# Later loads of elements 1 to 3 held behind the first weight matrix, element 1's keys on GpSimd's queue, and a new order for every engine

## The chip, the cores and the metric

The kernel runs on one core of one Trainium2 chip. The metric is the device time of one execution in microseconds (us); the time of the kernel before is the median of three executions, 109.86 us (109.25 to 112.44). One execution was also recorded by the hardware profiler; the times inside a run are counted from the start of its span.

The core has TensorE (PE, matrix products; PEld is its loading of weights), VectorE (DVE), ScalarE (ACT), GpSimd (POOL) and SyncE (SP, which here only issues transfers). Each engine takes its own instructions strictly in their written order. Transfers are issued from SP, ACT and POOL and are carried by the same 16 DMA engines.

## What is computed

Four batch elements, four heads, 1088 positions, head size 32. Polynomial attention without a softmax, then a two-layer network on the 4352 resulting rows:

```python
def phi(x):                                   # 32 -> 64 features
    a = np.einsum('rd,bhsd->bhsr', S1, x)     # r = 8
    b = np.einsum('rd,bhsd->bhsr', S2, x)
    return np.einsum('bhsi,bhsj->bhsij', a, b).reshape(*x.shape[:-1], r * r)
kv  = np.einsum('bhsf,bhsd->bhfd', phi(k), v)
z   = np.sum(phi(k), axis=2)
num = np.einsum('bhsf,bhfd->bhsd', phi(q), kv)
den = np.einsum('bhsf,bhf->bhs', phi(q), z)[..., None] + 1e-06
x   = (num / den) as rows [4352, 128]         # heads side by side
out = np.maximum(x @ w_in, 0.0) ** 2 @ w_out  # 128 -> 2048 -> 128
```

## The kernel before, in words

**The work and its names.** Every piece of work is an `op` of a small planner in the kernel file (class `Plan`), with a name, an engine (or two that could do it), a modelled duration and what it reads and writes. For the four elements b = 0 to 3:

- `ld kin_x.b`, `ld qin_x.b`, `ld vin_x.j` load keys, queries and values. Each of the three has two buffers, so element 2 reuses element 0's. Element 0 comes in pieces (`ld k0.0`, `ld k0.1`, `ld k0.r`, `ld q0.0` to `.2`, `ld vin_0.0` to `.3`, `.r0`, `.r1`); elements 1 to 3 have one transfer of 544 KB for the keys, one for the queries, and four for the values. In this text k1, q1 and v1.0 to v1.3 are those of element 1, and so on.
- `kT`, `K1`, `kab`, `kp`: keys transposed (DVE), multiplied with S1 and S2 (PE), turned back (DVE), and the 64 products per position formed in five pieces `kpb.0` to `.8` (POOL or DVE). `z`, `zs`, `Wc_ps`, `Wc` make the denominator's weights, `kvb.0` to `.8` the sum over positions, `kvs`, `KVT`, `KV4T`, `KV` bring it into shape.
- `qT`, `qpr`, `qpc`, `qa`, `qc`, `ac`, `den`, `rec`, `a'`, `qo`, `qd` do the same for the queries, scaled by one over the denominator; `x...` (PE) multiplies them with the sum and `xT...` copies the result, in bf16, to where the network reads it.
- The network runs over ten chunks of rows: `0a` and `0b` of 256 rows, `1` to `7` of 512, `8` of 256 (the two last positions of every group). A chunk is 8 groups of `F1 n.g` (x @ w_in, PE), `relu n.g` (ACT, a few on DVE), 4 of `sq n.g2` (square, DVE, a few on ACT) and 4 of `F2 n.g2` (@ w_out, PE); the 256-row chunks have half as many, each as large. `osb` copies the result out of PSUM and `st o...` stores it. Chunks 0a, 0b and 1 need element 0, chunks 2 and 3 element 1, 4 and 5 element 2, 6 and 7 element 3.

**What sets the order.** `ORDER` is a list of the numbers of all ops, written out by hand (found by a search), and `ALT` names the ops that run on their second engine. `Plan.run` walks the list with its modelled durations only to give out the PSUM buffers (two of two banks, `h`; four of one bank, `t`); each engine then executes its ops in the order of the list, and waits on the chip are set by the data. A real extra wait comes only where `behind` is set: the transfer is then not issued before the named one has landed (line 971). A load's `reads=["gate"]` orders it in the planner alone.

**The places that the change touches.** `load_whole` (line 288) loads the keys and queries of elements 1 to 3, all from SP, with no `behind`. `load_v` (line 294) loads the values; those of element 1 come from POOL, those of 2 and 3 from SP (`loads`, line 930). w_in and w_out (line 364 and the next) are loaded on POOL, after the copy `gate` (line 363), which waits for `ld q0.0`. They are read as f32 (1 MB each) and land as bf16 (512 KB). Line 109 and those around it model a transfer's landing, lines 891 to 903 store chunks 0a and 0b, 0a in four transfers (`HALVES`).

**The order around the start**, decoded from the list, up to the first network chunks:

```
SP    ld k0.0 | k0.1 | k0.r | q0.0 | v0.0 | v0.1 | v0.2 | q0.1 | q0.2 | k1 | k2 | q1 | v2.1 | k3 | q2 | ...
POOL  ... S2r | v0.r0 | v0.r1 | gate | ld w_in | kp0.2 | S2b | kp0.4 | ld v1.0 | kp0.8 | ld v1.3 | ld w_out |
      ld v1.2 | ld v1.1 | a'1 | qo1.0 | qo1.1 | kp1.2 | kp1.6 | kp1.4 | kp1.8 | kp2.2 | kp1.0 | ...
DVE   m4 | kT0.0 | m2 | Wab | W4 | kT0.1 | kab0.0 | kT0.r | kab0.1 | E1 | kab0.r | qT0.0 | mh | kp0.0 | kp0.6 | zs0 |
      qo0.0 | qT0.1 | qT0.2 | ac0.0 | den0.0 | qTr0 | rec0.0 | kvs0 | kT1 | ac1 | den1 | rec1 | xT0.0 | kab1 | kT2 |
      zs1 | qd1.0 | Wc1 | qd1.1 | qT1 | kab2 | xT1.A | ...
PE    S12T | K1 0.0 | K1 0.1 | K1 0.r | z0 | qpr0.0 | kv0.0 | kv0.2 | Wc_ps0 | kv0.4 | c0.0 | kv0.6 | qpr1.0 | kv0.8 |
      qpr1.2 | qoT0.0 | qpr1.4 | KVT0 | R0.0 | x0.0 | K1 1 | KV4T0 | F1 0a.2 | F1 0a.0 | z1 | F1 0a.1 | Wc_ps1 |
      F1 0a.3 | K1 2 | x1 | qpce1 | qpre1 | F1 0b.1 | F2 0a.0 | F1 0b.0 | F2 0a.1 | ... | xe1 | F1 1.6 | F2 1.0 |
      F1 1.7 | F1 1.4 | kv2.0 | ...
ACT   ... | qa0.0 | Wc0 | kvs40 | qp0.0 | qab1 | KV0 | Rs0.0 | KV40 | relu 0a.2 | relu 0a.0 | relu 0a.1 | relu 0a.3 |
      sq 0a.0 | sq 0a.1 | relu 0b.1 | relu 0b.0 | osb0a | relu 0b.3 | relu 0b.2 | sq 0b.1 | ...
```

Ahead of the first `F1` the PE also runs filler products (line 962), put in where the planner sees idle time.

Of the kernel before, what the change touches and what calls it, by code (L numbers as in the profile page):

```python
# [23 lines left out]


HOP, FIX, TAIL, SWITCH = 0.06, 1.4, 0.6, 0.1
RATE = 235.0
OVER = {"PE": 0.15, "DVE": 0.08, "ACT": 0.1, "POOL": 0.03}


class Plan:
# [35 lines left out]
    def run(self, slots, t0=0.7):  # L67
        free = {e: t0 for e in ("PE", "ACT", "DVE", "POOL", "SP")}
        held = {"DVE": [], "POOL": []}
        dmat = {}  # L70
        lane = {"HW": [], "SW": []}
        pool = {kind: [(0.0, (kind, i)) for i in range(n)] for kind, n in slots.items()}
        users, last, was = {}, {}, False
        for o in self.ops:
            for t in o.uses:
                users[t] = users.get(t, 0) + 1
        assert sorted(ORDER) == list(range(len(self.ops)))
        self.order = [self.ops[i] for i in ORDER]
        for o in self.order:
            e, d = o.eng[ALT.get(o.n, 0)]  # L80
            full = o.name[0] == "F"
            s = free[e] + (SWITCH if e == "PE" and full != was else 0.0)
            was = full if e == "PE" else was
            for p in o.preds:
                s = max(s, p.end + (HOP if p.eng[0][0] != e or p.dma is not None else 0.03))
            for t in o.allocs:
                x = min(pool["h"] + pool["t"] if t.kind == "r" else pool[t.kind])
                t.kind, t.i = x[1]
                pool[t.kind].remove(x)
                s = max(s, x[0] + HOP if x[0] else 0.0)  # L90
            if e in o.port:
                other = held["DVE" if e == "POOL" else "POOL"][-14:]
                if e == "POOL" and held["DVE"]:
                    s = max(s, held["DVE"][-1][1] + HOP)
                near = 0.06 if e == "DVE" else 0.0
                while any(a <= s + near and s < b - 1e-9 for a, b in other):
                    s = next(b for a, b in other if a <= s + near and s < b - 1e-9)
                held[e].append((s, s + d))
            if o.dma is not None:
                l = lane["SW" if e == "POOL" else "HW"]  # L100
                s = max(s, l[-8] if len(l) > 7 else 0.0)
                if e == "POOL":
                    held[e].append((s, s + 0.75 * d))
            o.eng, o.start, o.end = [(e, d)], s, s + d
            free[e] = s + d - (OVER.get(e, 0.0) if o.dma is None else 0.0)
            if o.dma is not None:
                q_, x_ = ("SW", "HW") if e == "POOL" else ("HW", "SW")
                begin = max(dmat.get(q_, 0.0), o.end + (FIX if o.pri is None else 1.0 if e != "POOL" else 2.2))
                shared = min(max(dmat.get(x_, 0.0) - begin, 0.0), 2 * o.dma) / 2
                dmat[q_] = begin + o.dma + shared  # L110
                dmat[x_] = dmat.get(x_, 0.0) + shared
                o.end = dmat[q_] + TAIL
                lane[q_].append(o.end)
            for t in o.uses:
                users[t] -= 1
                last[t] = max(last.get(t, 0.0), s + d)
                if users[t] == 0:
                    pool[t.kind].append((last[t], (t.kind, t.i)))
        return self.order
# [8 lines left out]
HOOK = {"1": ("0a", 3), "e1": ("1", 4), "e2": ("3", 4), "e3": ("5", 4), "8": ("6", 4)}  # L128
FINE = ("8",)
FILL = 0.12  # L130
HALVES = ("0a",)
ORDER = [
# [21 lines left out]
]  # L154
ALT = {
# [3 lines left out]
}  # L159


# [1 line left out]
def kernel(  # L163
# [33 lines left out]
    S2r = T("S2r", [128, D])  # L197
# [10 lines left out]
    w_in = T("w_in", [128, d_ff], BF16)  # L208
# [36 lines left out]
    P = Plan()  # L245
# [33 lines left out]
    def rows(x, b):  # L279
        return x[b].rearrange("h (t j) d -> (h t) j d", j=NJ)  # L280
# [4 lines left out]
    def keys3(rg, b):  # L285
        return [f"{rg(b)[1]}.{x}" for x in ("0", "1", "2" if rg is qin else "r")]

    def load_whole(x, b, rg):
        t, key = rg(b)
        load("SP", f"ld {key}.{b}", t, rows(x, b), 557, keys3(rg, b), ["gate"])  # L290

    JK = [0, 9, 18, 26]

    def load_v(b, eng):
        t, key = vin(b)
        vr = v[b].rearrange("h (t j) d -> t h j d", j=NJ)
        for j4 in range(4):
            j0, n = (8 * j4, 8) if b == 0 else (JK[j4], 9 if j4 < 2 else 8)
            l = load(eng if isinstance(eng, str) else eng[j4], f"ld {key}.{j4}", t[32 * j4 : 32 * j4 + 32, :, :n, :].rearrange("p h m d -> p h (m d)"),
                 vr[:, :, j0 : j0 + n, :].rearrange("t h m d -> t h (m d)"), 16.4 * n,  # L300
                 [f"{key}.{j4}"] + ([f"{key}.r{j4}"] if n == 9 else []), ["gate"] if b else [f"{K0k}.0"] if j4 == 3 else [], first=b == 0)
            if b == 0 and j4 == 3:
                l.behind = P.w[f"{K0k}.0"]
        if b == 0:
            for g in range(2):
                load("POOL", f"ld {key}.r{g}", t[32 * g : 32 * g + 32, :, 8, :], vr[:, :, 32 + g, :], 16, [f"{key}.r{g}"], first=True)
# [623 lines left out]
    def loads(b):  # L930
        if b < B:
            load_whole(k, b, kin)
            load_whole(q, b, qin)
            load_v(b, "POOL" if b == 1 else "SP")

    first_part(x0, "x0.0")
    token_major("1")
# [64 lines left out]
```

## Time and profile before

| | |
|---|---|
| Median of three executions | 109.86 us (109.25 to 112.44) |
| The profiled execution, its own time | 110.45 us |
| its span, from first to last instruction | 107.9 us |
| granted TensorE clock, mean | 0.99 |
| busy: PE / DVE / ACT / POOL | 97.8 / 89.4 / 80.0 / 29.9 us |
| DMA: moved in all | 10.22 MB, mean 95 GB/s |
| first F1 product | at 17.50 us |
| last F2 product ends | at about 102.1 us |

How to read it: the view by groups has, for each line of the kernel and shape, the busy time, the mean of one, and the idle time ahead of it with what ended it. The timeline gives start and duration in time order; a row with several instructions gives the time from the first one's start to the last one's end. The chain of waits follows the work that ended last back through what released each step. In the view of the DMA queues, the hardware queue q1 is SP's, q10 is ACT's, and the software queue q0 is POOL's. A matmul's duration is that of one pipelined product, so the time of a group on PE is read from its neighbours' starts.

### The profile page before, as it was taken

How to read it: one execution, taken by the hardware profiler on the slowest of the kernel's cores; microseconds unless marked ns; L12 is line 12 of the kernel's file. 1: busy time of each engine (PE TensorE's matmuls, PEld its weight loads, DVE VectorE, ACT ScalarE, POOL GpSimd, SP SyncE). 2: the span in 40 equal slices, each digit the busy share in tenths (PEclk: the TensorE clock that was granted, in tenths of full speed). 3: DMA queues.
4: the chain of work that ended last, by engine and by line, in shares of the span. 5: the costliest groups of instructions: out<-in, count | busy, mean ns of one | idle time of the engine just before them, and what ended most of it. 6: DMA issues, size and time to landing. Idle time of an engine off the chain costs nothing.

```text
span 107.9 us, 3883 instructions
## 1 busy us (share of the span) xinstructions
PE 97.8 (91%) x1676; PEld 71.9 (67%) x1676; DVE 89.4 (83%) x137; ACT 80.0 (74%) x99; POOL 29.9 (28%) x44
## 2 busy tenths in 40 slices
PE   7886999799999998999999999999999999999800
PEld 5545776549777575666886786788568688889600
DVE  1588479899999799979998998998889999979600
ACT  3230063999999988979999699999887799678600
POOL 7339906999189562000003000000000000000000
PEclk9999999999999999999999999999999999999996
DMA  1999999991029921000000122000032001200242
GB/s 37 255 211 337 308 304 233 301 282 61 6 74 223 260 70 51 0 6 3 0 0 6 55 79 67 0 6 0 7 87 82 0 0 51 76 0 11 80 110 52
DMA packets 9360, 10.22 MB, mean 95 GB/s; under 512 B 848, under 2 KB 8064, under 8 KB 9344
## 3 DMA queue, kind: packets, MB, share of 16 engines
q1 hardware_dynamic: 8448, 8.13, 26.8%
q0 software_dynamic: 576, 1.66, 6.9%
q10 hardware_dynamic: 320, 0.20, 1.0%
q8 instruction: 13, 0.21, 0.8%
q14 instruction: 3, 0.02, 0.1%
HBM read 8.80 MB, written 2.23 MB: 102 GB/s over the span
## 4 chain that ended last, share of the span: by engine, by line
PE 63%; ACT 14%; DMA 8%; DVE 5%; issue 3%; ACTq 0%
PE h L801 22%; PE t L837 21%; ACT r L813 10%; PE t L448 6%; DMA vin<-in_v_dram 5%; DMA kin<-in_k_dram 3%; PE h L652 2%; DVE g L826 2%; ACT osb L268 2%; ACT g L826 2%; PE h L553 2%; PE h L486 1%; PE h L680 1%; PE t L684 1%; ACT r L807 1%
## 5 line engine op out<-in xcount | busy, mean ns | idle before, releaser
L813 ACT ACTIVATE r<-h 128x1024 bf16<-128x1024 f32 x63 | 61.3, 1024 | 6.8 <-PE h L801 6.4
L837 PEld LDWEIGHTS <-g 128*128 128x128 bf16 x544 | 33.1, 98 | 5.5 <-DVE g L809 0.3
L837 PE MATMUL t<-w_out,g 128*128 128x128 bf16 x544 | 36.0, 219 | 0.1
L826 DVE TENSOR_TENSOR g<-r 128x2048 bf16<-128x2048 bf16 x29 | 34.5, 1206 | 0.8 <-ACT r L813 0.5
L801 PE MATMUL h<-xT,w_in 128*128 128x512 bf16 (+1 forms) x112 | 29.8, 370 | 0.6 <-ACT r L813 0.4
L801 PEld LDWEIGHTS <-w_in 128*128 128x128 bf16 x160 | 18.7, 148 | 7.8 <-issue 4.2
L499 POOL TENSOR_TENSOR kp<-kab 128x512 f32<-128x512 f32 x12 | 12.6, 1073 | 17.0 <-DVE g L826 17.0
L633 DVE STREAM_TRANSPOSE qd<-qo 128x1024 f32<-128x1024 f32 (+1 forms) x7 | 7.9, 1144 | 0.0
L448 PE MATMUL t<-kp,vin 128*32 128x64 f32 (+1 forms) x288 | 6.9, 223 | 1.1 <-DMA vin<-in_v_dram 0.9
L826 ACT ACTIVATE g<-r 128x2048 bf16<-128x2048 bf16 x4 | 7.6, 1922 | 0.1
L448 PEld LDWEIGHTS t<-kp,vin 128*32 128x32 f32 (+1 forms) x288 | 4.8, 109 | 4.2 <-issue 2.0
L962 PE MATMUL t<-const-bfloat16-1.0 128*128 128x256 bf16 x35 | 6.7, 326 | 0.8 <-PEq L986 0.8
L801 PE MATMUL h<-x0r,w_in 128*128 128x256 bf16 (+1 forms) x32 | 6.7, 333 | 0.0
L652 PE MATMUL h<-qd,KV 32*32 32x256 f32 (+2 forms) x160 | 6.3, 342 | 0.2 <-ACT r L813 0.2
L652 PE MATMUL t<-qd,KV 32*32 32x256 f32 (+2 forms) x160 | 6.5, 343 | 0.0
L814 DVE TENSOR_SCALAR r<-h 128x1024 bf16<-128x1024 f32 x4 | 4.9, 1224 | 1.1 <-PE h L801 0.7
L962 PEld LDWEIGHTS <-const-bfloat16-1.0 128*128 128x128 bf16 x35 | 3.7, 118 | 2.4 <-issue 1.3
L652 PEld LDWEIGHTS h<-qd,KV 32*32 32x32 f32 x160 | 3.4, 103 | 2.2 <-ACT r L813 0.7
L718 DVE TENSOR_TENSOR qo<-qaq,qaf 128x1024 f32<-128x1024 f32 x4 | 4.7, 1218 | 0.0
L479 DVE STREAM_TRANSPOSE kT<-kin 128x1088 f32<-128x1088 f32 x3 | 3.9, 1287 | 0.0
L526 DVE STREAM_TRANSPOSE qT<-qin 128x1024 f32<-128x1024 f32 x3 | 3.6, 1204 | 0.0
L268 ACT COPY osb<-t 128x512 f32<-128x512 f32 (+2 forms) x6 | 2.7, 466 | 0.9 <-PE t L837 0.9
(125 smaller groups left out, 99.8 us busy)
## 6 DMA issues: line engine op xcount, KB each, us to landing
out_dram<-osb SPq DMA_DIRECT2D x29, 64.0 KB
kin<-in_k_dram SPq DMA_DIRECT2D x3, 544.0 KB
qin<-in_q_dram SPq DMA_DIRECT2D x3, 544.0 KB
vin<-in_v_dram SPq DMA_DIRECT2D x7, 128.0 KB
vin<-in_v_dram SPq DMA_DIRECT2D x4, 144.0 KB
kin<-in_k_dram SPq DMA_DIRECT2D x2, 256.0 KB
w_in<-in_moe_w_in_dram POOLq DMA_DIRECT2D x1, 512.0 KB, 10.2
w_out<-in_moe_w_out_dram POOLq DMA_DIRECT2D x1, 512.0 KB, 10.2
```

Source lines behind the costliest of these rows:

```text
L268: op(e, 0, lambda en: act.copy(o(), i()) if en == "ACT" else dve.tensor_copy(o(), i()), reads, writes, name)
L448: pe.matmul(pb(tv)[32 * h : 32 * h + 32, :64], V[:Pn, h, m, :], kp_[:Pn, m, h].rearrange("p i j -> p (i j)"), start=(m == 0), stop=(m == 8 ...
L499: return (pool if e == "POOL" else dve).tensor_tensor(out=kp_[:, 2 * u : 2 * u + 2].rearrange("p m h i j -> p (m h) i j"), in0=x, in1=y, o ...
L633: op("DVE", DVT(256 * G), lambda e: dve.transpose(qd_[:, g0 : g0 + G].rearrange("p g f t -> p (g f t)"), qo_[:, :G].rearrange("p g h x y - ...
L652: pe.matmul(bank[32 * h : 32 * h + 32, :n], KV4[rg if b is None else b][rows, y, 32 * h : 32 * h + 32], qd_[rows, :G, 2 * h + y, :], start ...
L718: return (pool if e == "POOL" else dve).tensor_tensor(out=qo_.rearrange("p g h i j -> p (g h) i j"), in0=x_, in1=y_, op=ALU.mult)
L801: pe.matmul(hv()[:, x], w_inv[:, ct], X, start=True, stop=True)
L813: lambda e, hv=hv, Rv=Rv, own=own: act.activation(Rv[:, own], hv(), ACTF.Relu) if e == "ACT"
L814: else dve.tensor_scalar_max(Rv[:, own], hv(), 0.0),
L826: lambda e, R=R, G=G: dve.tensor_mul(G, R, R) if e == "DVE" else act.activation(G, R, ACTF.Square),
L837: pe.matmul(tb[o.i][:, x : x + 128], Gv[:, y, tt * 128 : tt * 128 + 128], w_out[:, ct], start=(ct == 0 and x == 0), stop=(ct == CT - 1), s ...
L962: pe.matmul(pb(fill)[:, :256], one.to_broadcast([128, 128]), one.to_broadcast([128, 256]), start=True, stop=True)
```

## The change

Four things change. (1) Element 1's keys go from SP's queue to POOL's, in the list between `gate` and `ld w_in`. (2) Every other later load of keys, queries and values (q1, v1, and all of elements 2 and 3) gets `behind = w_in`: the queue that issues it stands until w_in has landed. v1.0 to v1.2 go from POOL's queue to SP's; v1.3 stays on POOL's. (3) The planner adds a measured lateness to the first loads' modelled landings, and chunk 0a's store goes out in two transfers in place of four. (4) `ORDER` and `ALT` are new.

```diff
+LATE = (("ld k0.r", 1.0), ("ld S2r", 1.0), ("ld q0.0", 0.6), ("ld vin_0.", 0.6), ("ld q0.1", 0.3))
...
-                o.end = dmat[q_] + TAIL
+                o.end = dmat[q_] + TAIL + next((x for a, x in LATE if o.name.startswith(a)), 0.0)
...
-HALVES = ("0a",)
+HALVES = ()
 ORDER = [
...
     def load_whole(x, b, rg):
         t, key = rg(b)
-        load("SP", f"ld {key}.{b}", t, rows(x, b), 557, keys3(rg, b), ["gate"])
+        l = load("POOL" if x is k and b == 1 else "SP", f"ld {key}.{b}", t, rows(x, b), 557, keys3(rg, b), ["gate"] if x is k and b == 1 else ["w_in"])
+        if x is not k or b > 1:
+            l.behind = P.w["w_in"]
...
-                 [f"{key}.{j4}"] + ([f"{key}.r{j4}"] if n == 9 else []), ["gate"] if b else [f"{K0k}.0"] if j4 == 3 else [], first=b == 0)
+                 [f"{key}.{j4}"] + ([f"{key}.r{j4}"] if n == 9 else []), ["w_in"] if b else [f"{K0k}.0"] if j4 == 3 else [], first=b == 0)
             if b == 0 and j4 == 3:
                 l.behind = P.w[f"{K0k}.0"]
+            elif b:
+                l.behind = P.w["w_in"]
...
-            load_v(b, "POOL" if b == 1 else "SP")
+            load_v(b, ("SP", "SP", "SP", "POOL") if b == 1 else "SP")
```

The new list, decoded in the same way:

```
SP    ld k0.0 | k0.1 | k0.r | q0.0 | v0.0 | v0.1 | v0.2 | q0.1 | q0.2 | (w_in landed) k2 | q1 | k3 | v1.0 | v1.1 | q2 |
      v2.3 | v1.2 | v2.0 | v2.2 | v3.0 | st o0a.0 | ...
POOL  ... S2r | v0.r0 | v0.r1 | gate | ld k1 | ld w_in | S2b | kp0.6 | ld w_out | kp0.8 | qo1.1 | qo1.0 | kp1.2 | kp1.4 |
      kp1.6 | kp1.0 | (w_in landed) ld v1.3 | kp2.6 | kp1.8 | kp2.4 | ...
DVE   m4 | m2 | kT0.0 | W4 | E1 | Wab | kT0.1 | mh | kab0.0 | kT0.r | kab0.1 | kab0.r | qT0.0 | kp0.0 | kp0.2 | zs0 | kp0.4 |
      qo0.0 | qT0.1 | qT0.2 | ac0.0 | den0.0 | rec0.0 | kT1 | ac1 | den1 | rec1 | a'1 | xT0.0 | qTr0 | kab1 | qd1.1 | qd1.0 |
      kT2 | zs1 | xT1.A | kab2 | qT1 | sq 0a.1 | zs2 | kT3 | ...
PE    S12T | K1 0.0 | K1 0.1 | K1 0.r | z0 | qpr0.0 | kv0.0 | Wc_ps0 | kv0.2 | kv0.4 | c0.0 | qpr1.0 | kv0.6 | qpr1.2 | kv0.8 |
      qpr1.4 | KVT0 | qoT0.0 | KV4T0 | R0.0 | x0.0 | K1 1 | F1 0a.1 | F1 0a.3 | z1 | F1 0a.0 | F1 0a.2 | x1 | K1 2 | F1 0b.2 |
      Wc_ps1 | z2 | F1 0b.0 | F2 0a.0 | ... | xe1 | F1 1.6 | F2 1.0 | F1 1.7 | F1 2.1 | F2 1.1 | F1 2.0 | kv2.0 | ...
ACT   ... | qa0.0 | Wc0 | kvs0 | kvs40 | qab1 | KV0 | qp0.0 | Rs0.0 | KV40 | relu 0a.1 | relu 0a.3 | relu 0a.0 | relu 0a.2 |
      sq 0a.0 | xT1.B1 | relu 0b.2 | xT1.B0 | Wc1 | relu 0b.0 | relu 0b.3 | sq 0b.1 | ...
```

Ops that change their engine. From ACT to DVE: sq 0a.1, sq 1.1, relu 5.4, 6.1 and 7.2, osb3, osb4, and seven smaller copies. From DVE to ACT: sq 1.0, relu 5.7, 6.3, 6.6 and 7.7, osb1, and eleven smaller copies (among them both `xT1.B`, Wc1, Wc2, kvs41, xTe1.A). From POOL to DVE: kp0.2, kp0.4, a'1, a'e2. From DVE to POOL: kp0.6, a'e1.1, qoe2.0, qoe3.0. PE's work is the same, in another order.

More of the change, by code (lines that the diff above doesn't have):

```diff
@@ L130 @@
 FILL = 0.12
-HALVES = ("0a",)
+HALVES = ()
 ORDER = [
[21 rows of a table removed]
[21 rows of a table added]
 ]
 ALT = {
[3 rows of a table removed]
+    36: 1, 37: 1, 42: 1, 103: 1, 108: 1, 128: 1, 151: 1, 170: 1, 177: 1, 187: 1, 188: 1, 231: 1, 251: 1, 272: 1, 289:
+    1, 302: 1, 331: 1, 347: 1, 351: 1, 353: 1, 366: 1, 382: 1, 385: 1, 396: 1, 413: 1, 423: 1, 438: 1, 450: 1, 490: 1,
 }
```

45 rows, old and new, of tables (ALT, ORDER) are left out of this document.

## The prediction

> **What bounds the kernel now.** I read the busy times by stretches first (which engine is full, and where is PE not), then the chain of waits (what the start hangs on), then w_in's and the queues' rows (what the moved loads collide with).
>
> Stretches; columns: PE, PEld, DVE, ACT, POOL busy, granted clock, DMA share, GB/s.
>
> ```profile
> 17.50:22.00 4.50, 3.60 (x53) 2.58 (x52) 4.20 (x7) 4.12 (x6) 4.49 (x4) 1.00 1.04 273
> 22.00:27.00 5.00, 4.99 (x126) 3.69 (x127) 4.76 (x9) 5.00 (x4) 5.00 (x6) 1.00 0.54 164
> ...
> 37.00:42.00 5.00, 4.73 (x122) 3.33 (x121) 4.90 (x9) 4.47 (x5) 2.29 (x3) 1.00 0.32 79
> ...
> 62.00:67.00 5.00, 5.00 (x85) 3.71 (x84) 4.73 (x5) 4.83 (x6) 0.00 (x0) 1.00 0.28 79
> ...
> 87.00:92.00 5.00, 5.00 (x70) 4.27 (x68) 5.00 (x6) 4.76 (x6) 0.00 (x0) 1.00 0.12 31
> ```
>
> PE, DVE and ACT are all nearly full from 22 us on, and DMA is idle late. Up to 24 us DMA is full.
>
> Chain of waits; start, duration, what:
>
> ```profile
> 3.90 5.76 DMA vin<-in_v_dram
> 9.66 0.25 issue
> 9.90 0.43 PE t L448 x16
> ...
> 12.64 0.62 PE h L553 x4
> 13.26 0.24 PE t L448 x8
> ...
> 15.98 0.35 PE t L535 x4
> ...
> 17.51 1.09 PE h L801 x8
> ...
> 52.04 0.88 PE h L801 x4
> 52.91 0.89 PE t L837 x16
> ```
>
> To 9.66 element 0's last values are on their way; then PE is busy almost without a gap to x0.0 (L535), xT0.0 ends at 17.11 (timeline of DVE: 16.69 + 0.42) and the first F1 runs at 17.5. The last two rows are the unit prices: two F1 groups 0.88, one F2 0.89.
>
> **How much there is to win.** There are 68 F1 groups (0.44 each, 29.9) and 34 F2 (0.89, 30.3). The rest of PE's work after 17.5, from the spacing of its rows: three z and Wc_ps (2.3), two K1 (1.3), four x stages (6.4), three qpc with qpr (3.5), three kv (4.2), three KV4T and qpr8 (1.6): 19.3. Together 79.5 us of the 84.6 between 17.5 and 102.1. Of the 5.1 left, 1.7 is the closing chain (99.55 to 102.1 less one F2), which the new order leaves as it is. So 3.4 us is all that any order can win after the first F1; about 2.4 of it lies ahead of 44 us.
>
> **The loads.** w_in:
>
> ```profile
> L275 POOL DMA_DIRECT2D w_in<-in_moe_w_in_dram x1: 570/570/570, 7.2 to 7.2; - x1
> ...
>   DMA w_in<-in_moe_w_in_dram: 0.3, 1
> ...
> DMA to landing us min/median/max: 10.2/10.2/10.2
> ```
>
> It lands at 7.22 + 10.2 = 17.4, and PE waits 0.3 us for it: no more hangs on it, since xT0.0 ends at 17.11. The queues between 7.2 and 11.4, then between 11.4 and 17.5:
>
> ```profile
> q1 hardware_dynamic: 521, 1.26, 95.9%
> q10 hardware_dynamic: 103, 0.09, 11.5%
> ```
>
> ```profile
> q0 software_dynamic: 248, 0.87, 64.6%
> q1 hardware_dynamic: 221, 0.84, 40.7%
> ```
>
> In the first stretch POOL's queue moves nothing: w_in's first packet comes 4.2 us after its issue. In the second it shares with k1, k2 and q1. From 10 to 11 us, when q1 alone runs, it moves 418 GB/s; in the second stretch, with w_in and w_out counted as they are read (f32, twice what lands), 2 x 0.87 + 0.84 MB in 6.1 us is 423 GB/s. So 544 KB costs 1.3 us and a weight matrix 2.5.
>
> After: k1 is issued on POOL in w_in's old place (7.2). Its landing has no row. From below: the small POOL loads land 4.2 and 4.4 us after issue (S2r, v0.r), so 11.6. From above: w_in's 10.2, so 17.4. I take w_in's first packet plus k1's own time and 0.3 for completion: 7.2 + 4.2 + 1.3 + 0.3 = 13.0, nearest to w_in because place and issue are the same, without the sharing, because SP issues nothing until w_in has landed. Who waits: kT1 (1.29) on DVE, placed ahead of ac1, and behind it den1, rec1, a'1, xT0.0. ac1's other input, qab1, comes at about 14.8 (below), so k1 may land until 13.5 at no cost. w_in, issued 0.57 later behind it, lands at 13.0 + 2.5 = 15.5 (from below 14.1), two us ahead of its use. w_out, now issued at about 10 (11.96 before), follows 2.5 later, and is first used after 24. SP then issues k2 at 15.5; beside w_out it lands between 18 (1.0 to start, 1.3, 0.3) and 20.5 (w_out's 2.5 first). kT2 is due at about 20.2. q1 and k3 follow 1.3 each, 19.5 to 22 and 21 to 23.5, due at 23.2 and 25.6; v1 by 28, due at 30. Behind the waiting SP are only later loads and stores; osb0a, the first store, is written after 32 us. Behind v1.3 on POOL is nothing that waits. The two store issues saved on SP (0.4 to 0.5 each) lie in SP's idle time: 0.
>
> On DMA descriptors the Trainium skill speaks against the move to GpSimd: "SBUF — State Buffer", section "SBUF: two separate sides", says that GpSimd writes the descriptors of its own transfers and is locked out while VectorE holds their shared port, and that a transfer from SP or ACT is immune. By that rule k1 would start later than from SP; w_in's 4.2 us agree that something holds this queue back, without showing what. Its consequence is the rival on the other side, below.
>
> **The start.** PE up to x0.0 has the same list but that qpr1.2 moves ahead of kv0.8 (+0.62) and KV4T0 ahead of x0.0 (+0.37); Wc_ps0 only changes place, and the fillers between (0.4) can go. From 9.90: kv0.8 ends at 13.7 (13.50), qpr1.4 at 14.3, qab1 on ACT (now ahead of qp0.0) at 14.8 (15.56), R0.0 at 16.0, x0.0 at 16.55 (16.55), xT0.0 at 17.0 (17.11). On DVE E1 and mh (0.45) leave the stretch ahead of kp0.0, and kp0.2, kp0.4 (0.63 each) come in for kp0.6: DVE has 1.1 us idle ahead of 12.4, which covers it. First F1 at 17.25 against 17.50: **-0.25**.
>
> **From the first F1 to 46 us.** a'1 leaves POOL (0.51 from 16.92) for DVE (about 0.36, as L560's row of this size) and is done at 16.1, so qo1.1 and qo1.0 (2 x 1.5) end at 19.2 on POOL, not 20.5, and qd1.0 on DVE (0.97) at 20.2, not 21.5. x1 starts when a two-bank buffer is free: 20.65, not 22.01. ACT is the full engine here (relus at 0.95 apiece back to back, squares 1.9): it loses sq 0a.1 and sq 1.1 (-3.8), takes sq 1.0 (+1.9) and six small copies (+1.9), gives one (-0.35): -0.35. DVE takes sq 0a.1 and sq 1.1 (+2.3) and gives sq 1.0, xTe1.A, both xT1.B, Wc1, Wc2, kvs41 (-3.2), with qT3 moved back by 1.2. Walked through by hand with these rows, two two-bank buffers and 0.05 per hand-over: F2 0a.0 at 24.2 (24.88), xe1 at 37.55 (37.02) with one more F1 done, and at 46.6 PE has one F1 and one F2 more behind it than before at 46.5, and one qpc (0.57) fewer: 0.44 + 0.89 - 0.57 - 0.1 = 0.65 ahead, the 0.25 included. The head start of x1 is thus mostly given back at xe1, where qd's halves and ACT's list decide. From below this step costs: the hand walk leaves out slips, and the chip's order may meet a buffer later. From above it wins the 2.4 us. I take **-0.4** on top of the start.
>
> **From 46 us to the end.** One relu fewer on DVE (-1.22), qoe2.0 and qoe3.0 to POOL (-2.4; POOL is idle there, 1.95 each), against a'e2, kvs42, osb3, osb4 and others (+3); ACT about even. PE loses only 1.0 us there now. I take **-0.3**. For what the walk leaves out, **+0.3**.
>
> **Sum.** -0.25 - 0.4 - 0.3 + 0.3 = -0.65. The profiled execution took 110.45 (span 107.9 and 2.55 around it), so 109.8; it lies 0.6 above the median, so 109.2 as a median.
>
> **Rivals.**
> 1. *Nothing is left (no change).* What PE gains at x1 it gives back at xe1 (the walk shows most of that), and k2 at 20.5 holds kT2, and with it xT1.A and F1 0b, by 0.3 to 0.4. For it: PE near full after 44. Against it: ACT and DVE both lose work. -0.25 - 0.4 fall away: 109.9, to 110.6 with k2's wait and slips.
> 2. *Clean.* The new order removes 2.5 of the 3.4 us: 109.86 - 0.25 - 2.5 = 107.1. For it: 1.3 us earlier x1, and less work on DVE. Against it: it needs three quarters of everything there is.
> 3. *Slower: k1 comes late on POOL's queue.* Place: kT1 on DVE, and everything behind it down to xT0.0. It decides from a landing at 13.5: each us later is a us at the first F1. At w_in's 10.2 us, 17.4: 3.9 later, 109.86 + 3.9 - 0.25 - 0.4 = 113.1; at 15.5, 111.2. For it: both 512 KB loads of this queue took 10.2, and two loads are now issued in a row. Against it: the sharing that made it so is gone, and my 13.0 is inside the limit, though by only 0.5.
>
> **How the numbers follow.** Forecast 0.42 (108.4 to 109.8), nothing 0.20, clean 0.18, k1 late 0.20 (111.2 to 113.1, most of it above 112.06). Within 2% (107.66 to 112.06, about what can be told from no change) lie the forecast, the second and the low end of the last: 0.64; faster 0.18; slower 0.18. The range of 106.9 to 112.4 leaves out the lower part of clean and the upper part of k1 late.
>
> **What would show it.** Right: kT1 starts by 13.8 with no DMA wait; w_in lands before 16; first F1 within 0.3 of 17.25; POOL's qo pair ends near 19.2; x1 before 21.2. Wrong: a DVE wait for kin at kT1 or kT2 of over 0.5 us; a first F1 after 18; new waits of DVE or POOL on each other after 46; or a PE gap in the steady part.

## The result, and the profile after

The changed kernel takes **108.66 us** (median of 7 executions, 108.18 to 108.91) against 109.67 for the kernel before in the same session. The ratio is **0.990, 95% interval 0.986 to 0.993**; in a repeat on another chip it was 0.994 (0.990 to 0.997). Disturbed executions are left out of every ratio, so a ratio need not be that of two medians. The gain is real and small: 0.6 to 1.0%.

The profiled execution of the changed kernel took 108.7 us, span 106.3. The stretches that the prediction showed, in the same columns:

```profile
17.50:22.00 4.50, 3.67 (x108) 2.52 (x109) 3.42 (x5) 4.50 (x5) 4.50 (x5) 1.00 0.99 310
22.00:27.00 5.00, 4.73 (x90) 3.45 (x74) 4.77 (x7) 4.46 (x8) 3.23 (x5) 1.00 1.05 208
37.00:42.00 5.00, 4.95 (x116) 3.07 (x102) 4.73 (x9) 4.66 (x5) 2.38 (x3) 1.00 0.33 101
62.00:67.00 5.00, 4.95 (x88) 4.05 (x87) 5.00 (x6) 4.45 (x6) 0.00 (x0) 1.00 0.26 75
87.00:92.00 5.00, 4.94 (x58) 4.06 (x59) 4.55 (x6) 4.03 (x5) 0.00 (x0) 1.00 0.20 56
```

In these stretches PE is nearly as full as before. In the one between them, 27 to 32 us, it is not (before first, then the changed kernel):

```profile
27.00:32.00 5.00, 5.00 (x128) 3.64 (x126) 4.75 (x13) 4.86 (x6) 2.21 (x3) 1.00 0.10 25
27.00:32.00 5.00, 3.99 (x86) 2.61 (x83) 4.61 (x9) 3.88 (x4) 1.86 (x3) 1.00 0.39 84
```

DMA is now full from 22 to 27 us as well (share 1.05 against 0.54): the held-back loads move there. The chain of waits (start, duration, what) shows the change in two places:

```profile
12.61 0.61 PE h L557 x4
13.47 0.63 PE h L557 x4
16.35 3.00 POOL qo L575 x2
19.37 0.99 DVE qd L579
...
29.72 1.01 issue
30.73 0.66 PE t L452 x32
```

POOL's pair qo1 runs from 16.35 to 19.35, about as forecast (19.2). But in the steady part PE now stands for 1.01 us ahead of `kv1.0` (L452), put down to "issue", that is, to nothing that the profile names. The two loads of POOL's queue, k1 and then w_in (issue, and time from issue to landing):

```profile
L275 POOL DMA_DIRECT2D kin<-in_k_dram x1: 582/582/582, 6.5 to 6.5; - x1
...
DMA to landing us min/median/max: 5.0/5.0/5.0
```

```profile
L275 POOL DMA_DIRECT2D w_in<-in_moe_w_in_dram x1: 570/570/570, 7.1 to 7.1; - x1
...
DMA to landing us min/median/max: 7.6/7.6/7.6
```

k1 lands at 11.6 and w_in at 14.8. DVE's kT1 and kT2 (timeline: start, duration, and in brackets any idle time ahead) wait for neither k1 nor k2:

```profile
12.38 0.20 DVE L627 RECIPROCAL den<-den 128x8 f32<-128x8 f32 x1
12.50 1.26 DVE L483 STREAM_TRANSPOSE kT<-kin 128x1088 f32<-128x1088 f32 x1
...
20.27 1.27 DVE L483 STREAM_TRANSPOSE kT<-kin 128x1088 f32<-128x1088 f32 x1
```

**Where the time went.** Three terms make up each profiled span: the first F1, from there to the end of the last output copy (osb8), and from that copy to the end, when the last stores land. Here they are for every kernel that was run; the lower ten are the experiments below. All values are in us, and the two kernels' repeats are called before_again and after_again.

| kernel | ratio to before (95%) | first F1 | F1 to last copy | copy to end | span |
|---|---|---|---|---|---|
| before | | 17.50 | 84.89 | 5.52 | 107.9 |
| before_again | | 16.75 | 84.64 | 5.38 | 106.8 |
| after | 0.990 (0.986 to 0.993) | 16.60 | 85.43 | 4.29 | 106.3 |
| after_again | 0.994 (0.990 to 0.997) | 16.74 | 85.03 | 4.42 | 106.2 |
| loads_alone | 1.044 (1.034 to 1.054) | 16.89 | 88.46 | 5.98 | 111.3 |
| no_hold_k1_sp | 0.983 (0.976 to 0.990) | 16.75 | 84.44 | 4.51 | 105.7 |
| no_hold_again | 0.986 (0.983 to 0.988) | 16.35 | 84.43 | 4.35 | 105.1 |
| v1_early | 0.991 (0.988 to 0.994) | 16.74 | 84.96 | 4.68 | 106.4 |
| k1_sp_hold | 0.993 (0.988 to 0.997) | 16.78 | 85.69 | 4.24 | 106.7 |
| fetch_clear | 0.990 (0.987 to 0.994) | 16.82 | 84.57 | 4.48 | 105.9 |
| before_osb6 | 0.993 (0.989 to 0.997) | 17.05 | 84.60 | 4.56 | 106.2 |
| after_osb6_back | 1.000 (0.997 to 1.004) | 16.16 | 85.15 | 5.58 | 106.9 |
| best_tail | 0.990 (0.987 to 0.992) | 17.33 | 84.40 | 4.50 | 106.2 |
| before_tail | 0.993 (0.990 to 0.995) | 16.91 | 84.67 | 4.41 | 106.0 |

Between the two kernels the middle term, where the prediction put its gain, grew (85.43 and 85.03 against 84.89 and 84.64). The gain is in the last term, 4.3 to 4.4 instead of 5.4 to 5.5, which the prediction had left as it was. The first term scatters: two profiles of one kernel differ by 0.75 (before), 0.14 (after) and 0.40 (no_hold).

### The profile page after: what moved, and what is told of

Read it like the earlier page. It is cut to its first block, busy times and chain, and to the rows that moved or that the text cites. A ratio compares the mean times of both kernels' runs of the same rounds, so it can differ in the third digit from the quotient of the medians.

```text
span 106.3 us, 3880 instructions
## 1 busy us (share of the span) xinstructions
PE 96.5 (91%) x1664; PEld 72.4 (68%) x1680; DVE 88.4 (83%) x134; ACT 79.4 (75%) x102; POOL 31.0 (29%) x42
## 4 chain that ended last, share of the span: by engine, by line
PE 68%; ACT 10%; DVE 8%; issue 5%; POOL 3%; ACTq 0%; DVEq 0%; POOLq 0%
PE h L805 22%; PE t L841 22%; ACT r L817 7%; PE t L452 5%; PE t L966 5%; PE h L656 4%; POOL qo L575 3%; DVE kp L413 2%; PE h L557 2%; PE t L656 2%; PE h L490 1%; PE h L684 1%; PE t L688 1%; ACT osb L268 1%; DVE g L830 1%
## 5 line engine op out<-in xcount | busy, mean ns | idle before, releaser
L817 ACT ACTIVATE r<-h 128x1024 bf16<-128x1024 f32 x64 | 62.3, 1023 | 10.6 <-PE h L805 8.2
L830 DVE TENSOR_TENSOR g<-r 128x2048 bf16<-128x2048 bf16 x30 | 35.9, 1215 | 2.8 <-PE t L841 1.5
L805 PE MATMUL h<-xT,w_in 128*128 128x512 bf16 (+1 forms) x99 | 28.0, 369 | 1.1 <-ACT r L817 0.5
L722 POOL TENSOR_TENSOR qo<-qaq,qaf 128x1024 f32<-128x1024 f32 x3 | 5.9, 1957 | 18.6 <-DVE g L830 18.6
L452 PE MATMUL t<-kp,vin 128*32 128x64 f32 (+1 forms) x288 | 6.9, 223 | 1.6 <-issue 1.0
L966 PE MATMUL t<-const-bfloat16-1.0 128*128 128x256 bf16 x39 | 7.2, 329 | 0.8 <-PEq L990 0.8
L452 PEld LDWEIGHTS t<-kp,vin 128*32 128x32 f32 (+1 forms) x288 | 4.8, 109 | 4.4 <-issue 3.5
L830 ACT ACTIVATE g<-r 128x2048 bf16<-128x2048 bf16 x3 | 5.7, 1909 | 0.0
L575 POOL TENSOR_TENSOR qo<-qaq,qab 128x768 f32<-128x768 f32 x2 | 3.0, 1515 | 6.0 <-DVE qaq L569 6.0
L818 DVE TENSOR_SCALAR r<-h 128x1024 bf16<-128x1024 f32 x3 | 3.7, 1222 | 0.9 <-PE h L656 0.7
L268 DVE COPY osb<-t 128x512 f32<-128x512 f32 (+1 forms) x6 | 3.7, 611 | 0.4 <-PE t L841 0.4
```

What stands on the lines that cost most here:

```text
L268: op(e, 0, lambda en: act.copy(o(), i()) if en == "ACT" else dve.tensor_copy(o(), i()), reads, writes, name)
L452: pe.matmul(pb(tv)[32 * h : 32 * h + 32, :64], V[:Pn, h, m, :], kp_[:Pn, m, h].rearrange("p i j -> p (i j)"), start=(m == 0), stop=(m == 8 ...
L575: return (pool if e == "POOL" else dve).tensor_tensor(out=qo6[:, 3 * y : 3 * y + 3].rearrange("p g h i j -> p (g h) i j"), in0=x_, in1=y_, ...
L722: return (pool if e == "POOL" else dve).tensor_tensor(out=qo_.rearrange("p g h i j -> p (g h) i j"), in0=x_, in1=y_, op=ALU.mult)
L805: pe.matmul(hv()[:, x], w_inv[:, ct], X, start=True, stop=True)
L817: lambda e, hv=hv, Rv=Rv, own=own: act.activation(Rv[:, own], hv(), ACTF.Relu) if e == "ACT"
```

## The experiments

The first question was which part of the change does what: the theory "the order earns the gain and the moved loads little", against "the loads earn it". The four kernels of the first group ran on one chip.

**before_again**: the kernel before, once more, unchanged.

> The kernel before, unchanged, for a second profile. Theory (the order wins): first F1 again at 17.3 to 17.7, w_in landing about 17.4, and 5 us or more from the last output copy to the end of the span. Rival (the profile compared with was a poor execution): element 0's first queries land at 6.4 rather than 7.0 as in the changed kernel, first F1 at or before 17.0, under 5 us after the last copy.

Measured 109.25 us, span 106.8, first F1 at 16.75. In the profile that the prediction was made from, element 0's first queries had landed at 7.04; here they landed at 6.31. So 0.7 us of that profile's 17.50 was its own late start, and this profile is the better one to set the others against. The rival was right in this; the theory was right that over 5 us pass behind the last copy (5.38).

**loads_alone**: the change's loads with the order of before.

```diff
 ORDER = [...]   # as before, but v1.3 and w_out trade places on POOL
...
+        l = load("POOL" if x is k and b == 1 else "SP", ...)
+        if x is not k or b > 1:
+            l.behind = P.w["w_in"]
...              # load_v as in the change
```

> The order of before, with only the loads changed: k1 on GpSimd's queue ahead of w_in, all other later loads behind w_in's landing, v1.3 issued after w_out. Theory (the order wins, the loads give little): w_in lands by 15.5, PE's 0.3 us wait for it goes, first F1 at 17.1 to 17.3, ratio to before 0.995 to 1.005, and values of element 1 landing at 28 to 30 may cost at kv1.0. Rival (the loads win): first F1 at 16.7 or earlier and ratio 0.985 to 0.992.

Measured 1.044, which neither side expected: the loads alone cost 4.8 us. DVE's waits, and PE's timeline, between 15 and 24 us:

```profile
DVE kT L483 <- DMA kin<-in_k_dram: 2.9, 1, 2.9
```

```profile
21.94 0.64 PE L441 MATMUL t<-zs,S2b 128*128 128x32 f32 x2 [2.66 <-DVE zs L437]
```

k2 now lands at 20.5 (14.7 in before_again). The old order has kT2 early on DVE, so DVE stands 2.9 us, zs1 and everything behind it are late, and PE stands 2.66. That is not the whole loss. Wc_ps1, where PE goes on, is 3.0 us later than in before_again (21.94 against 18.95), but kv1.0 is 4.45 us later (32.23 against 27.78), although PE has no further wait worth naming between them. In this stretch the granted clock (the third number from the right) was halved, in loads_alone and not in before_again:

```profile
22.00:27.00 5.00, 5.00 (x94) 2.36 (x94) 4.00 (x6) 3.54 (x3) 3.19 (x5) 0.50 1.04 238
22.00:27.00 5.00, 5.00 (x101) 3.85 (x90) 4.72 (x10) 4.96 (x5) 4.44 (x5) 1.00 0.41 127
```

The clock was at 0.50 from 20.8 to 27.7, beginning while PE stood, and x1 took 1.88 us instead of 1.21. The other three runs of loads_alone have the same mean clock over the span (0.961 to 0.969 in all four, 0.997 in before_again). That the standing brought the low clock on is likely but not shown by a run of its own. So about 3 us are the wait for k2 and about 1.4 the clock behind it. The hold on w_in thus cannot live without the new order, which puts kT2 at 20.3. Whether the hold earns anything with it was the next question.

**no_hold_k1_sp**: the changed kernel with its new order, but with k1 on SP and nothing held.

```diff
-        l = load("POOL" if x is k and b == 1 else "SP", f"ld {key}.{b}", ...)
-        if x is not k or b > 1:
-            l.behind = P.w["w_in"]
+        l = load("SP", f"ld {key}.{b}", ...)
...
-            elif b:
-                l.behind = P.w["w_in"]
```

> The new order without the hold: nothing waits for w_in, k1 back on SyncE's queue. Theory (the order wins): w_in lands at 16 to 17.5 and holds the first F1 to that, so 0.5 to 0.9 us of the start goes, but values of element 1 land before 25 and PE's 1.0 us wait at kv1.0 goes: ratio to before 0.988 to 0.996. Rival (the loads win): 0.998 to 1.005.

Measured 107.76 us, ratio 0.983: the fastest of all, and the repeat gave 0.986 (below). First F1 is at 16.75, though w_in lands at 16.7 instead of 14.8. PE's timeline ahead of kv1.0, of the repeat first and then of the changed kernel:

```profile
28.92 0.39 PE L801 MATMUL h<-x0r,w_in 128*128 128x512 bf16 x1
29.45 0.65 PE L448 MATMUL t<-kp,vin 128*32 128x64 f32 x32
```

```profile
29.33 0.39 PE L805 MATMUL h<-x0r,w_in 128*128 128x512 bf16 x1
30.73 0.48 PE L452 MATMUL t<-kp,vin 128*32 128x64 f32 x19 [1.01 <-issue]
```

Nearly all of the difference of the two kernels (0.9 of the 1.0 us in the middle term) arises at this one place and is carried to the end. So the new order earns the gain (which part of it does is tested below), and the loads take a part of it back. What is late at 29.7?

**v1_early**: the changed kernel with element 1's values brought forward.

```diff
-  SP   ... k2 | q1 | k3 | v1.0 | v1.1 | q2 | v2.3 | v1.2 | ...
-  POOL ... kp0.8 | qo1.1 | ... | kp1.6 | kp1.0 | ld v1.3 | ...
+  SP   ... k2 | q1 | k3 | v1.0 | v1.1 | v1.2 | q2 | v2.3 | ...
+  POOL ... kp0.8 | ld v1.3 | qo1.1 | ... | kp1.6 | kp1.0 | ...
```

> The changed kernel with v1.2 issued right behind v1.1 and v1.3 on GpSimd's queue as soon as w_in has landed, not behind kp1.0. Theory: the last value of element 1 lands by 26 rather than 30.4, PE's wait of 1.0 us ahead of kv1.0 goes, and 0.5 to 1.0 us of it reaches the end: ratio to before 0.980 to 0.985. Rival (the wait is taken back later, because ACT and DVE hold PE anyway): ratio 0.987 to 0.991, like the changed kernel.

Measured 0.991, no better than the changed kernel, though all of v1 had landed by 26.2: the rival's number, but not its reason. kv1.0's wait was gone, but PE now stood in the middle of a group of F2, where nothing is waited for:

```profile
28.24 1.00 PE L841 MATMUL t<-w_out,g 128*128 128x128 bf16 x15
29.79 0.22 PE L841 MATMUL t<-w_out,g 128*128 128x128 bf16 x1 [0.55 <-issue]
```

In the trace of the transfers one thing fits: the queue that brings the engines' instructions (q8 in the view of the DMA queues, 16 KB in one packet). In the kernels without late loads its third packet starts at 24.0 (before_again) or 25.8 (no_hold_k1_sp); here it starts at 27.1 and at 27.8 in the changed kernel, where the DMA engines are full with loads. The second group tested this, GpSimd's queue, and the tail.

**k1_sp_hold**: the changed kernel with only k1 back on SP; the rest stays held.

```diff
-        l = load("POOL" if x is k and b == 1 else "SP", f"ld {key}.{b}", ...)
+        l = load("SP", f"ld {key}.{b}", ...)
```

> The changed kernel with only element 1's keys back on SP's queue; the later loads still wait for w_in. Theory (the hold on w_in is what costs the 0.85 us, by the gap of TensorE near 29.7): like the changed kernel, the gap of 0.5 to 1.0 us near 29.7 is still there, ratio 0.989 (0.985 to 0.994). Rival (GpSimd's queue costs it): no gap, ratio 0.983.

Measured 0.993, with a gap of 1.40 at the same place: the theory. It is the hold that brings the gap, not GpSimd's queue.

**fetch_clear**: the changed kernel with q2 and v2.0, v2.2, v2.3 held until v1.3 has landed. In the list these four move behind v1.3, so v1.2 now follows v1.1 directly.

```diff
 ORDER = [...]   # q2, v2.3, v2.0, v2.2 behind v1.3
...
-            l.behind = P.w["w_in"]
+            l.behind = P.w[f"{vin(1)[1]}.3"] if x is q and b == 2 else P.w["w_in"]
...
-                l.behind = P.w["w_in"]
+                l.behind = P.w[f"{vin(1)[1]}.3"] if b == 2 else P.w["w_in"]
```

> The changed kernel with element 2's queries and first three value pieces held further, until element 1's last value piece has landed (near 26), so that the transfers pause near 25 and go on until about 30 to 31. Theory (TensorE's gap near 29.7 is a late fetch of its instructions: the 16 KB packet of the instruction queue starts at 27.8 behind the data of the loads, and the gap ends 1.55 us behind its end): the packet starts by 26, the gap is below 0.1 us, x of element 2 comes 0.8 earlier, ratio 0.982 (0.977 to 0.988). Rival (the gap is a late operand or a semaphore that the profile doesn't name): the gap stays within 0.3 of 1.0 us, ratio 0.989 or more.

In the trace it came out as expected: the packet starts at 24.08, the gap is gone, and the middle term is 84.57, as without the hold. In the time it did not show: the ratio of 0.990 (0.987 to 0.994) is that of the changed kernel and only touches what was expected (0.982, 0.977 to 0.988), though the profile has no gap. Where the time went instead stays open. And the edit cleared two things at once, for v1.3 landed at 26.5 instead of 30.4. Which of them held PE can be read from the semaphore instructions of PE's weight-load queue at kv1.0 (min/median/max ns, first and last start), in the changed kernel and in fetch_clear:

```profile
L452 PEldq EVENT_SEMAPHORE  x2: 51/668/1285, 29.1 to 29.2; - x2
```

```profile
L452 PEldq EVENT_SEMAPHORE  x2: 51/51/51, 29.3 to 29.4; - x2
```

In the changed kernel the second one, from 29.16, took 1.285 us, to 30.45. v1.3 had landed at 30.42 by the trace of the transfers. So **the values were late**, and the "issue" of the chain hides a wait for a transfer. In after_again it is the same: 905 ns, to 30.21, with v1.3 landed at 30.17. kv1.0's first weights are then loaded at 30.47, but the other 31 only from 30.74. There, and in the other kernels that stand here, PE's queue goes on 1.46 to 1.62 us behind the end of the instruction packet: after 29.16 to 30.74, after_again 28.86 to 30.45, after_osb6_back 28.34 to 29.96, k1_sp_hold 29.38 to 30.84, v1_early 28.29 to 29.79. (In k1_sp_hold 30.84 is the start of the two semaphore instructions, which then hardly wait, since v1.3 lands at 30.86; the first product follows at 31.13.) So two things are late within 0.3 us of each other, the values and the instructions, and the later one sets the end: v1_early removed the first, met the second, and won nothing that could be measured. That the packet was the cause in v1_early is argued from these five agreements; no run delayed it alone.

**before_osb6** and **after_osb6_back**: the tail. On DVE the changed kernel copies chunk 6's output (osb6) ahead of the last square of chunk 7, the kernel before copies it behind. Each experiment swaps the two.

```diff
 DVE  (before_osb6)
-     ... sq 7.2 | sq 7.3 | osb6 | ...
+     ... sq 7.2 | osb6 | sq 7.3 | ...
 DVE  (after_osb6_back)
-     ... sq 7.2 | osb6 | sq 7.3 | ...
+     ... sq 7.2 | sq 7.3 | osb6 | ...
```

> The kernel before with one swap in its order: VectorE copies chunk 6's output (osb6) ahead of its last square of chunk 7 instead of behind it. Theory (the tail's gain is SP's row of stores): chunk 6's four stores are issued 0.7 to 1.7 us earlier, the last landing and the end come 0.8 to 1.0 earlier while the last output copy stays at 101.4; ratio to the kernel before 0.991 (0.986 to 0.996). Rival (the tail's gain comes with the whole order, and this copy only trades places): ratio 1.000, copy to end stays 5.4.

> The changed kernel with the same swap undone: osb6 behind the last square of chunk 7 again. Theory: it gives the tail's gain back, copy to end 5.2 to 5.5 instead of 4.3, span about 107.2, ratio 0.998 (0.994 to 1.002). Rival: ratio stays at 0.990.

Measured 0.993 (0.989 to 0.997) and 1.000 (0.997 to 1.004): both as the theory had it. One swap in the old order gives most of what the whole change gives, and the changed kernel without it is no faster than before. DVE's timeline, first of before_again, then of the changed kernel (L826 and L830 are the squares):

```profile
95.51 1.22 DVE L826 TENSOR_TENSOR g<-r 128x2048 bf16<-128x2048 bf16 x1
96.65 0.68 DVE L268 COPY osb<-t 128x512 f32<-128x512 f32 x1
97.46 1.23 DVE L826 TENSOR_TENSOR g<-r 128x2048 bf16<-128x2048 bf16 x1
```

```profile
94.76 1.22 DVE L830 TENSOR_TENSOR g<-r 128x2048 bf16<-128x2048 bf16 x1
95.89 0.68 DVE L268 COPY osb<-t 128x512 f32<-128x512 f32 x1
96.49 1.22 DVE L830 TENSOR_TENSOR g<-r 128x2048 bf16<-128x2048 bf16 x1
```

In before_again the square ahead of the copy (95.51) is chunk 7's last and the one behind it chunk 8's first; in the changed kernel chunk 7's last (96.49) stands behind the copy. So the copy starts 0.76 earlier, 95.89 against 96.65, although the changed kernel's last output copy ends 0.64 later (102.03 against 101.39). What hangs on the copy is SP's row of stores. The DMA share in 40 slices from 103.0 to 106.3 us, of before_again and of the changed kernel:

```profile
DMA  4355579887878877882323232222200000000000
```

```profile
DMA  2234668875477974332322100000000000000000
```

The last packets go out at about 105.4 and 105.0. Between 97 and 102 SP's queue sends the rows of 512 bytes at 0.8 us for each 64 KB, and it issues a store each 0.58 us. Chunk 6's four stores, chunk 7's four and o8.0 stand in one line, so what is issued late in the line is sent late at its end.

**The last group** ran on a third chip: the changed kernel (after_again), the kernel without the hold (no_hold_again), and an attempt at a better tail, with the new order (best_tail, on no_hold_again) and with the old one (before_tail, on before_osb6, the moved store also one place up in the list). A second queue was to send beside the first.

```diff
-                    load("SP", f"st o{nm}.{x}", o[j], osv[:, x], 128, [], [ok])
+                    load("ACT" if (nm, x) == ("7", 3) else "SP", f"st o{nm}.{x}", o[j], osv[:, x], 128, [], [ok])
```

> The changed kernel once more, on the chip that runs the next three. Theory: ratio to the kernel before 0.990 (0.986 to 0.994), TensorE stands 0.5 to 1.0 us near 29.7, and its queue's wait for element 1's values there ends within 0.1 of the last value piece's landing. Rival (the gap was chance): no gap above 0.2.

> The changed kernel without the hold on w_in and with element 1's keys on SP's queue, once more. Theory (the hold brings element 1's last value piece and a fetch of TensorE's instructions late, for 0.85 us): no gap near 29.7, 0.6 to 1.0 us below after_again, ratio 0.983 (0.978 to 0.987). Rival (the earlier difference was that of two chips): within 0.3 us of after_again.

> As no_hold_again, and the last of chunk 7's four stores issued from ScalarE's queue in place of SP's. Theory (at the end one queue sends its 512-byte rows at 0.8 us for each 64 KB, and a second queue sends beside it): the last landing 0.6 to 0.9 earlier, copy to end 3.7 to 3.9, ratio 0.976 (0.971 to 0.982). Rival (the rows are limited by the transfer engines, whatever the queue, or the issue delays ScalarE's last copy): ratio as no_hold_again, 0.983.

> The kernel before with nothing of the change but osb6 ahead of the last square of chunk 7, and the last store of chunk 7 on ScalarE's queue. Theory (apart from the tail the searched order is worth only about 0.2 us): ratio 0.985 (0.980 to 0.990), 0.2 to 0.6 us behind best_tail. Rival (the order earns much of its time in the steady part): 1 us or more behind best_tail.

The first two came out as expected: 0.994 with a gap of 0.59 us, and 0.986 without one; their intervals (0.990 to 0.997, and 0.983 to 0.988) do not touch. best_tail fell: 0.990, and copy to end is 4.50 against 4.35. (In its profile most of the 1.1 us of longer span lies in the first F1, 17.33 against 16.35, which the edit doesn't touch; in the medians it is 0.5 us behind.) before_tail is no better than before_osb6 (0.993 both). The DMA queues from 99 to 102 us in best_tail:

```profile
q1 hardware_dynamic: 428, 0.21, 25.8%
q10 hardware_dynamic: 14, 0.01, 1.5%
issues: line engine op xcount, KB each, median us to landing
out_dram<-osb SPq DMA_DIRECT2D x4, 64.0 KB
out_dram<-osb ACTq DMA_DIRECT2D x2, 64.0 KB
```

ScalarE's store was issued at 99.56, but by 102.0 only 14 of its 128 packets had been sent; the first went out at 101.6, and until then SP's queue went on at its old pace. From 102.0 to 102.5 it was the other way round:

```profile
q10 hardware_dynamic: 78, 0.04, 27.0%
q1 hardware_dynamic: 2, 0.00, 0.2%
```

ScalarE's queue now sent at the old pace of SP's, and SP's sent next to nothing, though two of its stores were still waiting. So the second queue sent in place of the first and not beside it. "DMA: Bandwidth & Descriptors" of the Trainium skill, section "Issuing engines are not separate DMA queues", states that transfers from different engines share the same 16 transfer engines, and that issuing from several saves only the issue time. The measured end agrees, but the sharing alone doesn't explain it, since the 16 engines were only 27% busy; and in no_hold_again the two queues did send side by side between 102.0 and 102.5 (90 packets and 84). What made them take turns stays open. Why the first packet took 2.0 us, where SP's queue needs about 1.2 for its first store, stays open.

## Why the prediction came out right, and where it was wrong

109.2 was forecast and 108.66 measured, inside the forecast's own range (108.4 to 109.8), with the sign right. That the sum fits is in part luck: in means of the two profiles of each kernel, the middle term came out 0.9 us worse than forecast (+0.5, 85.23 against 84.77, not -0.4) and the end, which was left as it was, 1.1 better, and the two nearly cancel.

- **"First F1 at 17.25 against 17.50: -0.25".** Right in direction. The four profiles with the old order and the old loads have 17.50, 16.75, 17.05 and 16.91 (mean 17.05), the nine with the new order 16.16 to 17.33 (mean 16.70): 0.35 less, with a scatter as large, so that no run shows the term by itself.
- **"1.3 us earlier x1".** 20.50 in the changed kernel, forecast 20.65. Against before_again (21.26) it is 0.76; the rest was the late start of the profile it was worked from. The qo pair ended at 19.35 (forecast 19.2).
- **"The head start of x1 is thus mostly given back at xe1".** Right: xe1 came at 37.96 (37.55 forecast, one more F1 done); without the hold it came at 37.09.
- **"-0.4", "-0.3", "+0.3" after the first F1.** Together -0.4. The order itself, without late loads, is worth -0.25: the middle term is 84.40 to 84.57 in four profiles with the new order and no gap, and 84.60 to 84.89 in four with the old. So their sum was mis-sized by little; the three by themselves were not measured.
- **"v1 by 28, due 30", and with it the loads at no cost: wrong, and the first step that failed.** v1.3 landed at 30.42 and 30.17, and PE's queue was ready for kv1.0 at 29.2. The landings were worked out for the loads one after the other from w_in's landing, but v1.2 stands behind q2 and part of v2, and v1.3 is issued only at 23.4, behind POOL's kp1 pieces, into a DMA that is full until 30.4. Without the hold it is issued as late (23.4 and 23.0), but lands at 28.4 and 29.0. Together with the instructions the lateness costs 0.6 to 1.0 us, so the middle term came out at +0.5 instead of -0.4. Among the signs named beforehand, "a PE gap in the steady part" was the one that showed it.
- **"The closing chain ..., which the new order leaves as it is": wrong, and the larger miss.** The working stopped at 102.1, the last F2. After the last copy another 5.4 us pass in the stores, and osb6's place in DVE's list decides over about 1 us of them (0.9 in the old order, 1.2 in the new). The two lists, compared to their ends, show the swap.
- **Rival 3 (k1 late on POOL's queue)** fell: k1 landed at 11.6, not 13.0. It was issued 0.7 us earlier than in the profile before (6.53), and its first packet left at 8.0, 1.5 us after issue and not 4.2; the transfer then took 3.5 us to its landing, beside SP's, and not 1.6 (1.3 and 0.3) alone. SP's own transfer of k1 in no_hold_k1_sp landed at 11.5. The rule of the Trainium skill quoted there ("SBUF — State Buffer", section "SBUF: two separate sides"), that VectorE can lock GpSimd out of writing its transfers' descriptors, left no trace that could be seen: from issue to landing k1 took 5.0 us on GpSimd's queue and 5.7 on SP's.
- **Rival 2 (clean, 107.1)** is in time near what the order gives when the hold is left out, 107.8 and 107.7, but not by its mechanism: the middle term fell by 0.2 and not by 2.5, and the rest is the tail and the start. **Rival 1** is in time what the changed kernel is without osb6's swap, 1.000; but what took the gain there was the gap at kv1.0, while k2, which the rival named beside xe1, held nothing.

In means of the table: start -0.35 and order -0.25 (against the four profiles with the old order), the gap that the hold brings +0.8 (85.25, the mean of the five with a gap, less 84.46), tail -1.1 (4.36 against 5.45, the changed kernel's two and the two of the kernel before): -0.9 in all, where 0.7 to 1.1 was measured.

## What to carry to other kernels

Follow the work to the last landing, not to the last product: here the largest term of a rewrite of 490 operations was one copy, 0.7 us long, that moved ahead of a square and let a row of stores begin earlier. A load that is held back for a more urgent one must be checked against the deadline of the last load behind it in the same row, with everything that was put between; here the urgent load (w_in) came 2 us earlier without moving the first F1 beyond its scatter (16.60 and 16.74 with the hold, 16.75 and 16.35 without), and the last one came 1.2 to 2 us later. The version to keep is the new order without the hold: 0.983 and 0.986 of the time before.

## What was not expected of the hardware

- A wait for a transfer can stand in the profile as "issue": it was a semaphore instruction of 1.285 us in PE's own weight-load queue, which the list of waits does not name. The view of one line's instructions shows it.
- The engines' instructions are fetched while the kernel runs: the trace of the transfers lists 13 packets of 16 KB beside the data, about 1 us each (0.9 to 1.5). With the held loads in full flow the third packet started 1.2 to 4.3 us later (27.0 to 28.1 in the five profiles with a gap and 27.3 in loads_alone, 23.8 to 25.8 in the eight others), and in those five PE's queue went on 1.46 to 1.62 us behind the packet's end. When the packet was asked for is not in the trace, so that the loads delayed it is argued.
- One queue's stores of 512-byte rows went out at 0.8 us for each 64 KB, from 98 to 102 us, with the transfer engines only 26 to 28% busy (q1's row above, 25.8% over 3 us); in best_tail a second queue did not add to it.
- In loads_alone PE stood 2.66 us and the granted clock was 0.50 for 6.8 us, from 20.8 to 27.7, beginning within that stand; about 1.4 us of that kernel's loss lies in this stretch and not in the wait itself.
